# Three stretches of a matmul-bound attention and expert kernel: the second unit's weight blocks earlier, the last unit's sums in another order, the result's last blocks in pieces

## The chip, the cores and the metric

The kernel runs on one core of a Trainium2 chip, all in float32. The metric is the time of one execution in microseconds (us), the median of several runs. PE is the TensorE engine, PEld its weight loads, DVE VectorE, ACT ScalarE, POOL GpSimd, SP SyncE, whose queue issues most transfers. All runs quoted here are of the fast state. Even so, the kernel before varies: 1200.2 to 1209.1 us over the calls. Each kernel is therefore compared with runs of the kernel before on the same chip in the same call.

## The reference

```python
# cut to what matters
for b in range(nb):                      # 12 chunks of 64 positions, 4 batches, 8 heads
    intra = (q_b @ k_b.T * lam ** (i - j) (i >= j)) @ v_b
    inter = (q_b * lam ** (pos + 1)) @ kv_state
    out_b = intra + inter
    kv_state = lam ** 64 * kv_state + (k_b * lam ** (63 - pos)).T @ v_b
x = out as (3072, 512)                   # rows by model width
p = domain_probs / sum
out = sum over the 4 experts e of  p[:, e] * (relu(x @ w1[e]) @ w2[e])
```

## The kernel before

The rows of x fall into 3 groups, with 4 experts each: 12 units of work. The first unit's products are formed directly as soon as the attention of the first group is done ("direct products", 56 to 92 us). From the second unit on, each product of x with w1 (line of pg) is interleaved with a product of the hidden values with w2 (line of q). The products are of Strassen's kind with seven terms M1 to M7, each fed with sums and differences of blocks. DVE and POOL make these operand sums; DVE also adds up PSUM banks ("evictions"), and PE can use a bank again only then.

Engines work through their queues in order. The program is written by a Python scheduler: `chores` are side jobs, of which `pump` takes one when its count of steps says that POOL is free. The place in the program where a chore is written settles where its instructions stand in every engine's queue.

```python
def load(n, names="qkv"):                       # one chunk of q, k, v
    ...
    for r in range(2):
        nc.sync.dma_start(out=to[:, :, r], in_=of[:, :, r])
lam_bc = consts.tile([P, H], FP32, name="lam_bc")
nc.scalar.dma_start(out=lam_bc[:], in_=lam.partition_broadcast(P))
... # DVE makes s_decay (8 scans) and q_decay (7 products) of lam_bc;
    # st = scores * s_decay feeds PE's product with v

stage = ctx.enter_context(tc.tile_pool(name="stage", bufs=8))   # operand tiles, tag "st"

def pump(pace=1.0, force=False):
    ...                                          # stores that are due
    begins = chores and (force or free[0] <= now[0])
    if begins:
        begin = free[0] = max(free[0], now[0] - 1)
        was = max(busy[0], now[0])
        chores.pop(0)()
        free[0] = max(free[0], begin + max(pace * (busy[0] - was), 1))

def own_x(m):        # second unit: x operands of product m, four sums on DVE
    ...
    for n, x, y, op in T_OPS:
        tt(nc.vector, b[n], b[x], b[y], op)
    keep_own(("x", 0, m), x_ops[0, MS.index(m)], pieces)      # store for later groups
def own(m):          # own_w1: the same for w1, on POOL
    fed[0, 1, m] = own_x(m), own_w1(m)

raws = [lambda n=n: raw_w1(1, n) for n in ("A11", "A12", "A21", "A22")]
chores.extend((*prepare_w2(1), *raws, pause(4), mine["M1"], sum_own("S1", "A21", "A22", ALU.add)))
...                  # then the direct products, with pump() in every step
chores.extend((
    mine["M5"], sum_own("S2", "S1", "A11"),
    pause_till(0, 4), mine["M6"], sum_own("S3", "A11", "A21"),
    pause_till(1, 4), mine["M2"], sum_own("S4", "A12", "S2"),
    pause_till(2, 4), mine["M7"], ... ))
...
def give(m, t, tags):                            # turns a block of the result back
    ...                                          # 4 transposes into one bank
    nc.scalar.copy(out=o[:], in_=p[:])
    nc.sync.dma_start(out=out[r:r + 256, ...], in_=...)
```

## Time and profile before

| | before |
|---|---|
| median of the first 3 runs | 1204.43 us (1203.54 to 1204.65) |
| span of the profiled run | 1202.6 us |
| PE busy | 1188.0 us (99%) |
| PE not busy | 14.6 us |
| granted clock | 1.00 from the first record at 6.90 us to 1201.56 us, but for one stretch of 0.5, 95.65 to 99.06 us |

A table of windows has a row for each stretch: its length, the busy time and the number of instructions of PE, PEld, DVE, ACT and POOL, the granted clock, the share of the transfer engines, GB/s. A timeline's row is start, duration, engine, line, what it makes of what, sizes, count; in brackets stands the idle time before it and what ended that. The prediction below shows the rows that matter.

In what follows "wait" also stands for a figure that I count from the start times of the matmuls: the distance to the next start less the usual one (0.216 us for 128x256). Both kernels have 6623 matmul records of the same shapes in the same order, so the n-th of one can be set against the n-th of the other. I call the difference of their starts the **offset**.

### The profile page before, as it was taken

What the parts mean: (1) busy time and instruction counts of PE and PEld (TensorE: products, weight loads), DVE (VectorE), ACT (ScalarE), POOL (GpSimd) and SP (SyncE); (2) the same over time, 40 slices, a digit from 0 to 9 for tenths busy, and PEclk for the clock granted to TensorE, in tenths of its full rate; (3) what the DMA queues carried; (4) which work ended last, traced back from release to release, by engine and by line L of the source; (5) the groups of instructions that cost most, each with busy time, mean ns of one, the idle gap of its engine ahead of it and who ended that gap; (6) DMA issues with size and microseconds to landing.
All of it is one profiled execution on the core that took longest, in us unless ns stands there. A gap on an engine that the chain in (4) does not pass through costs nothing.

```text
span 1202.6 us, 17908 instructions
## 1 busy us (share of the span) xinstructions
PE 1188.0 (99%) x6623; PEld 1031.2 (86%) x6623; DVE 793.2 (66%) x1318; ACT 261.9 (22%) x476; POOL 635.3 (53%) x600
## 2 busy tenths in 40 slices
PE   9999999999999999999999999999999999999988
PEld 8887888888888888888888888888888888888877
DVE  6597796477467656746755774764665667777774
ACT  3321122112112201311220120120133341241232
POOL 1874267355468800044425745416675774874873
PEclk9999999999999999999999999999999999999999
DMA  9874869999989985789987999898987566566542
GB/s 224 231 262 166 276 208 352 352 315 332 377 286 328 339 286 173 224 286 275 283 286 233 304 311 319 278 315 304 301 280 262 215 229 248 218 241 227 208 151 71
DMA packets 227447, 317.94 MB, mean 264 GB/s; under 512 B 91648, under 2 KB 168864, under 8 KB 227360
## 3 DMA queue, kind: packets, MB, share of 16 engines
q1 hardware_dynamic: 219920, 314.63, 77.6%
q10 hardware_dynamic: 7440, 2.17, 0.8%
q8 instruction: 52, 0.85, 0.3%
q14 instruction: 35, 0.29, 0.1%
HBM read 231.40 MB, written 85.34 MB: 263 GB/s over the span
## 4 chain that ended last, share of the span: by engine, by line
PE 90%; DVE 3%; SPq 3%; DMA 2%; POOL 1%; issue 1%; ACT 0%; DVEq 0%; POOLq 0%
PE pg L733 38%; PE q L787 33%; PE pq L958 12%; DVE m L95 2%; SPq L122 2%; PE sp L484 1%; PE op L512 1%; POOL w2o L95 1%; PE op L507 1%; PE qp L461 1%; PE kp L461 1%; PE pM L928 1%; DMA probs<-in_moe_domain_probs_dram 1%; DMA w1b<-in_moe_w_dram 1%; PE op L520 1%
## 5 line engine op out<-in xcount | busy, mean ns | idle before, releaser
L733 PE MATMUL pg<-xs_in,ws_in 128*128 128x256 f32 x1960 | 470.3, 380 | 0.7 <-DVE m L95 0.5
L733 PEld LDWEIGHTS pg<-xs_in,ws_in 128*128 128x128 f32 x1960 | 370.5, 190 | 53.9 <-DVE m L95 2.5
L95 DVE TENSOR_TENSOR m<-pg,m 128x512 f32<-128x512 f32 x451 | 307.7, 687 | 111.7 <-PE pg L733 101.5
L787 PE MATMUL q<-w2t,hS 128*128 128x256 f32 x1024 | 243.3, 380 | 0.0
L787 PEld LDWEIGHTS q<-w2t,hS 128*128 128x128 f32 x1024 | 192.9, 190 | 26.8 <-issue 0.3
L803 DVE SCALAR_TENSOR_TENSOR acc<-q,gate,acc 128x256 f32<-128x256 f32 x192 | 92.4, 481 | 174.0 <-PE q L787 173.1
L787 PE MATMUL q<-w2t,m 128*128 128x256 f32 x768 | 183.9, 383 | 0.0
L787 PEld LDWEIGHTS q<-w2t,m 128*128 128x128 f32 x768 | 145.9, 191 | 20.6 <-issue 0.2
L745 ACT ACTIVATE m<-m 128x512 f32<-128x512 f32 x132 | 83.0, 630 | 337.1 <-DVE m L95 335.3
L95 POOL TENSOR_TENSOR m<-m,xT 128x512 f32<-128x512 f32 x64 | 81.6, 1290 | 78.4 <-ACT m L745 46.3
L95 POOL TENSOR_TENSOR kn<-kn,s_decay 128x512 f32<-128x512 f32 x20 | 22.1, 1105 | 170.4 <-PE kp L461 130.3
L95 DVE TENSOR_TENSOR sums<-pq,sums 128x256 f32<-128x256 f32 x154 | 64.1, 421 | 49.3 <-PE pq L958 41.7
L958 PE MATMUL pq<-acc,w2t 128*128 128x256 f32 x352 | 86.7, 379 | 1.9 <-POOL acc L95 1.9
L741 ACT COPY m<-pg 128x512 f32<-128x512 f32 x88 | 51.4, 585 | 154.6 <-PE pg L733 147.9
L95 DVE TENSOR_TENSOR m<-m,m 128x512 f32<-128x512 f32 x96 | 81.0, 847 | 0.0
L95 POOL TENSOR_TENSOR ops<-w2b 128x256 f32<-128x256 f32 x24 | 18.9, 807 | 109.6 <-DMA w2b<-in_moe_w_dram 109.6
L958 PEld LDWEIGHTS pq<-acc,w2t 128*128 128x128 f32 x352 | 66.8, 190 | 11.3 <-issue 2.2
L680 ACT ACTIVATE m<-m 128x512 f32<-128x512 f32 x48 | 30.3, 631 | 154.0 <-DVE m L95 154.0
L95 DVE TENSOR_TENSOR hS<-m,m 128x512 f32<-128x512 f32 x64 | 54.8, 861 | 8.4 <-ACT m L745 8.4
L95 POOL TENSOR_TENSOR acc<-hT,hT 128x512 f32<-128x512 f32 x32 | 40.1, 1270 | 32.5 <-DVE hT L95 19.5
L95 POOL TENSOR_TENSOR w2o<-w2b 128x512 f32<-128x512 f32 x32 | 41.8, 1326 | 24.2 <-DMA w2b<-in_moe_w_dram 21.4
L95 POOL TENSOR_TENSOR acc<-hT,acc 128x512 f32<-128x512 f32 x32 | 40.7, 1271 | 5.0 <-PE pq L958 2.7
(129 smaller groups left out, 1325.5 us busy)
## 6 DMA issues: line engine op xcount, KB each, us to landing
xs_in<-x_ops SPq DMA_DIRECT2D x70, 896.0 KB, 6.0
ws_in<-w_ops SPq DMA_DIRECT2D x70, 896.0 KB, 8.6
w2t<-w_ops SPq DMA_DIRECT2D x66, 256.0 KB, 6.6
w2t<-w_sums SPq DMA_DIRECT2D x64, 256.0 KB, 3.8
w_ops<-ops SPq DMA_DIRECT2D x28, 512.0 KB, 5.4
w2t<-in_moe_w_dram SPq DMA_DIRECT2D x48, 256.0 KB, 3.3
x_ops<-ops SPq DMA_DIRECT2D x17, 512.0 KB, 6.8
w2b<-in_moe_w_dram SPq DMA_DIRECT2D x32, 256.0 KB, 5.7
```

The source lines that it names most:

```text
L95: eng.tensor_tensor(out=o, in0=a, in1=b, op=op)
L122: nc.sync.dma_start(out=to[:, :, r], in_=of[:, :, r])
L461: nc.tensor.transpose(out=x[:, ac * C:(ac + 1) * C], in_=y[:, 2 * ac:2 * ac + 2].rearrange("p r d -> p (r d)"), identity=ident[:],)
L484: nc.tensor.matmul(out=sp[r][:, ac * C:(ac + 1) * C], lhsT=hc(kT)[half[r], ac], rhs=hc(qT)[half[r], ac], start=True, stop=True,)
L507: nc.tensor.matmul(out=op[r][half[x], a * C:(a + 1) * C], lhsT=kv[half[r], 2 * a + x], rhs=hc(qs)[half[r], 2 * a + x], start=(a == 0), sto ...
L680: nc.scalar.activation(out=o[:], in_=o[:], func=AF.Relu)
L733: nc.tensor.matmul(out=p[:, j * 256:(j + 1) * 256], lhsT=ws[i][:, j * P:(j + 1) * P], rhs=xs[i], start=(fresh and j == 0), stop=True, skip ...
L741: nc.scalar.copy(out=new[at][:], in_=p[:])
L745: nc.scalar.activation(out=new[at][:], in_=new[at][:], func=AF.Relu)
L787: nc.tensor.matmul(out=p[:, s * DH:(s + 1) * DH], lhsT=h[A_OF[m]][:, c * 256 + s * P:c * 256 + (s + 1) * P], rhs=fed2[g, e, m][uu][:, c], ...
L803: nc.vector.scalar_tensor_tensor(out=o, in0=x, scalar=w, in1=o, op0=ALU.mult, op1=ALU.add)
L958: nc.tensor.matmul(out=p[:, 0:256], lhsT=fed3[e, m, x // 2][:, x % 2, c * P:(c + 1) * P], rhs=b[B_OF[i]][:, c * 256:(c + 1) * 256], start= ...
```

## The change

The intent: the blocks of w1 for the second unit are asked for during the attention, so that its first product doesn't wait at 92 us; the last unit's operand sums are made in an order that fits its short products; the last blocks of the result go out in smaller pieces. With it comes a fourth edit: half of the first q and k loads go to ACT's queue, and lam_bc is asked for behind them.

```diff
@@ part A: load, lam_bc
                 for r in range(2):
-                    nc.sync.dma_start(out=to[:, :, r], in_=of[:, :, r])
+                    by = nc.scalar if n < 2 and r == 1 else nc.sync
+                    by.dma_start(out=to[:, :, r], in_=of[:, :, r])
-    lam_bc = consts.tile([P, H], FP32, name="lam_bc")
-    nc.scalar.dma_start(out=lam_bc[:], in_=lam.partition_broadcast(P))
...
+    lam_bc = consts.tile([P, H], FP32, name="lam_bc")
     for n, names in ((0, "qk"), (1, "qk"), (0, "v"), (2, "qk"), (1, "v"), (3, "qk")):
         load(n, names)
+        if (n, names) == (1, "qk"):
+            nc.scalar.dma_start(out=lam_bc[:], in_=lam.partition_broadcast(P))
@@ part B1: second unit (cut: the tiles of block A21 and of sum S1 also leave the stage buffers)
-            chores.extend(prepare_w2(0))
+            chores.extend((*prepare_w2(0), *(raw[n] for n in ("A11", "A22", "A21"))))
...
-    chores.extend((*prepare_w2(1), *raws, pause(4), mine["M1"], sum_own("S1", "A21", "A22", ALU.add)))
+    chores.extend((
+        mine["M1"], sum_own("S1", "A21", "A22", ALU.add), *prepare_w2(1), raw["A12"],
+    ))
@@ part B2: last unit (cut)
+        for part in names:            # outer sums: T1 of all blocks first, then T3 and T2
+            for at in BLOCKS:
...
+            b[name] = small("h" + name) if (e, m) == EARLY else opool.tile([P, W], FP32, name="acc")
...
-                elif ahead or x % 2 == 0:
+                elif ahead or x % 2 == 0 and x + i:
                     rest()
@@ part C: result (cut)
-    def give(m, t, tags):
+    def give(m, t, tags, dds=(0, 1)):
...
-    "M4": (("M5", 0), ("M5", 1), ("M2", 0), ("M2", 1), ("M4", 0))
+    "M4": (("M5", 0), ("M5", 1), ("M2", 0), ("M2", 1), ("M4", 0, (1,)), ("M4", 1, (1,)))
-    give("M4", 1, ("s1",))
+    give("M4", 0, ("q01",), (0,))
+    give("M4", 1, ("q11",), (0,))
```

More of the change, by code (lines that the diff above doesn't have):

```diff
@@ L333, in raw_w1 @@
         i, j = int(name[1]) - 1, int(name[2]) - 1
-        if name == "A22":
+        if name in ("A21", "A22"):
             to = tuple(small("w1b")[:] for _ in range(2))
@@ L344, in sum_w1 @@
     def sum_w1(e, name, a, b, op):
-        if e == 0:
+        if e == 0 or name == "S1":
             to = tuple(small("w1o")[:] for _ in range(2))
@@ L440, in take @@
         for x, f in enumerate(queue):
-            if force or getattr(f, "at", 0) <= now[0]:
+            if force or getattr(f, "at", 0) <= now[0] and getattr(f, "can", lambda: True)():
                 queue.pop(x)()
@@ L617, in total, with inner_sums @@
             outer[e][name][at] = o
-        work = []
-        for at in BLOCKS:
-            for n in names:
-                a, _ = of[n]
-                k = len(work)
-                if n in ("T1", "T3", "T4"):
-                    x = lambda a=a, at=at, tag={"T1": "s0", "T3": "s1", "T4": "s" + "01"[k % 2]}[n]: bring(a, at, tag)
-                    if not work:
-                        work.append([x])
-                    else:
-                        work[-1].append(x)
-                work.append([lambda n=n, at=at: total(n, at)])
-        background.extend(after(6, lambda fs=fs: [f() for f in fs]) for fs in work)
-    def inner_sums(e, m):
+        work, tags = [[]], itertools.cycle(("s0", "s1"))
+        for part in names:
+            for at in BLOCKS:
+                for n in part:
+                    if n != "T2":
+                        work[-1].append(lambda a=of[n][0], at=at, tag=next(tags): bring(a, at, tag))
+                    work.append([lambda n=n, at=at: total(n, at)])
+        background.extend(after(4 + 2 * (i > 4), lambda fs=fs: [f() for f in fs]) for i, fs in enumerate(work))
+    EARLY = E - 1, "M3"
+    def inner_sums(e, m, behind=False):
+        if (e, m) in within:
+            return
         blk, b = outer[e][B_OF[m]], {}
@@ L642, in total @@
                 b.update({"B" + at: blk[at] for at in BLOCKS})
-            b[name] = opool.tile([P, W], FP32, name="acc")
+            b[name] = small("h" + name) if (e, m) == EARLY else opool.tile([P, W], FP32, name="acc")
             tt(nc.gpsimd, b[name][:], b[x][:], b[y][:], ALU.subtract)
-        aside[0:0] = [lambda n=n, x=x, y=y: total(n, x, y) for n, x, y, _ in T_OPS]
+        work = [after(0, lambda n=n, x=x, y=y: total(n, x, y)) for n, x, y, _ in T_OPS]
+        for f in work:
+            f.can = lambda: len(blk) == 4
+        if behind:
+            aside.extend(work)
+        else:
+            aside[0:0] = work
     SEQ = ("M1", "M5", "M6", "M2", "M7", "M3", "M4")
@@ L690, in keep @@
             if g == LAST:
-                outer_sums(e, *{(0, 1): ("T1", "T3", "T2"), (1, 0): ("T4",)}.get((i, j), ()))
+                outer_sums(e, *{(0, 1): (("T1",), ("T3", "T2")), (1, 0): (("T4",),)}.get((i, j), ()))
                 return
@@ L904, in give @@
         p, o = bank(tags[t % len(tags)], "yp"), small("y")
-        for dd in range(2):
+        w = len(dds) * P
+        for x, dd in enumerate(dds):
             for s in range(2):
                 nc.tensor.transpose(
-                    out=p[:, s * DH + dd * P:s * DH + (dd + 1) * P], in_=sums[m][:, 2 * dd + t, s * P:(s + 1) * P],
+                    out=p[:, s * w + x * P:s * w + (x + 1) * P], in_=sums[m][:, 2 * dd + t, s * P:(s + 1) * P],
                     identity=ident[:],
                 )
-        nc.scalar.copy(out=o[:], in_=p[:])
-        r = LAST * G + j * W + t * 256
+        nc.scalar.copy(out=o[:, 0:2 * w], in_=p[:, 0:2 * w])
+        r, d = LAST * G + j * W + t * 256, i * DH + dds[0] * P
         nc.sync.dma_start(
-            out=out[r:r + 256, i * DH:(i + 1) * DH].rearrange("(s p) d -> p s d", p=P),
-            in_=o[:].rearrange("p (s d) -> p s d", s=2),
+            out=out[r:r + 256, d:d + w].rearrange("(s p) d -> p s d", p=P),
+            in_=o[:, 0:2 * w].rearrange("p (s d) -> p s d", s=2),
         )
@@ L1074 @@
     blocks = {}
+    raw = {n: lambda n=n: raw_w1(1, n) for n in ("A11", "A12", "A21", "A22")}
     m1, m2 = (direct_product(0, m, blocks, ("g1", "g3")) for m in ("M1", "M2"))
@@ L1134, in sum_own @@
         return lambda: sum_w1(1, name, a, b, op)
-    raws = [lambda n=n: raw_w1(1, n) for n in ("A11", "A12", "A21", "A22")]
-    chores.extend((*prepare_w2(1), *raws, pause(4), mine["M1"], sum_own("S1", "A21", "A22", ALU.add)))
+    chores.extend((
+        mine["M1"], sum_own("S1", "A21", "A22", ALU.add), *prepare_w2(1), raw["A12"],
+    ))
     for m in SEQ0[2:]:
@@ L1167 @@
     fill3 = [(e, m, k) for e in range(E) for m in SEQ3 for k in range(4)]
-    after_last = {"M2": (None,) * 5 + (("M3", 0), ("M3", 1)), "M4": (("M5", 0), ("M5", 1), ("M2", 0), ("M2", 1), ("M4", 0))}
+    after_last = {
+        "M2": (None,) * 5 + (("M3", 0), ("M3", 1)),
+        "M4": (("M5", 0), ("M5", 1), ("M2", 0), ("M2", 1), ("M4", 0, (1,)), ("M4", 1, (1,))),
+    }
     steps = attention(1)
@@ L1201 @@
             if nests and i == 6:
-                inner_sums(ahead[1], SEQ3[0])
+                inner_sums(ahead[1], SEQ3[0], nested)
+                if ahead[1] == EARLY[0]:
+                    inner_sums(*EARLY, True)
             a = []
@@ L1228 @@
                     if y:
-                        give(*y, ("s0", "s1"))
+                        give(*y[:2], ("s0", "s1"), *y[2:])
                 if x == 0 and at * 7 + i >= 6 and fill:
```

## The prediction

> **What bounds the kernel now.** I read the busy line first, then the waits of TensorE (PE), then a table of windows, then timelines of the stretches that the change touches. The page's busy line:
>
> ```profile
> PE 1188.0 (99%) x6623; PEld 1031.2 (86%) x6623; DVE 793.2 (66%) x1318; ACT 261.9 (22%) x476; POOL 635.3 (53%) x600
> ```
>
> and three rows of the waits (us in total, times, longest):
>
> ```profile
> PE pg L733 <- DVE ops L95: 2.9, 1, 2.9
> PE pq L958 <- POOL acc L95: 1.9, 1, 1.9
> PE yp L907 <- DVE sums L95: 1.2, 2, 0.6
> ```
>
> PE is busy for 1188.0 of a span of 1202.6 us. So **all waiting of PE together is 14.6 us**, 1.2% of the time; only a change of the matmuls, or of their clock, could bring more. The order listing shows PE's instructions in the same order in both kernels, 6623 of them, so the matmul work stays. 2% of 1204.43 is 24.1 us, which is more than all that could be saved.
>
> Where the 14.6 us lie, by windows (length, then busy time of PE, PEld, DVE, ACT, POOL, then granted clock, DMA share, GB/s):
>
> ```profile
> 0.00:20.00 20.00, 18.94 (x209) 17.43 (x210) 14.79 (x31) 7.27 (x13) 4.95 (x10) 1.00 0.92 223
> 60.00:80.00 20.00, 20.00 (x94) 17.61 (x93) 19.86 (x24) 1.17 (x2) 15.68 (x12) 1.00 0.88 310
> 80.00:100.00 20.00, 17.13 (x73) 14.44 (x72) 18.04 (x29) 8.44 (x14) 11.13 (x8) 0.91 0.46 149
> 1140.00:1160.00 20.00, 17.05 (x77) 13.97 (x76) 15.78 (x32) 7.44 (x13) 14.69 (x13) 1.00 0.52 190
> 1180.00:1200.00 20.00, 17.54 (x96) 14.84 (x94) 9.94 (x19) 6.78 (x12) 3.91 (x4) 1.00 0.26 92
> ```
>
> The idle time is at the start (1.06 us), at 80 to 100 us (2.87), at 1140 to 1160 (2.95) and at the end (2.46, and the 2.6 after 1200 us). The change works on just these. In 80 to 100 the clock is 0.91 as well, so that window loses more than its idle time. The timeline of PE there (start, us, out<-in, idle before):
>
> ```profile
> 89.36 1.89 PE L787 MATMUL q<-w2t,m 128*128 128x256 f32 x8
> 91.08 1.03 PE L733 MATMUL pg<-xT,w1b 128*128 128x256 f32 x4
> 94.98 1.40 PE L733 MATMUL pg<-ops 128*128 128x256 f32 x4 [2.87 <-DVE ops L95]
> 96.17 3.32 PE L787 MATMUL q<-w2t,m 128*128 128x256 f32 x8
> ```
>
> Eight matmuls of one kind took 1.89 us before the gap and 3.32 after it; start to start, 91.08-89.36 = 1.72 us against 99.33-96.17 = 3.16 (99.33 is the start of the next group). With the four of 94.98 I count **1.7 us lost to the clock after 2.87 us of idle time**. The operands come late because VectorE (DVE) has no idle time from 57 to 97 us and runs its queue in order:
>
> ```profile
> 94.42 0.75 DVE L95 TENSOR_TENSOR ops<-xT 128x256 f32<-128x256 f32 x2
> ```
>
> At the start, the lines that decide are of DVE, and PE's first product that needs them:
>
> ```profile
> 3.85 2.63 DVE L380 TENSOR_TENSOR_SCAN s_decay<-lam_bc,ident 128x128 f32<-128x128 f32 x8 [2.86 <-DMA lam_bc<-in_lam_dram]
> 6.76 3.43 DVE L393 TENSOR_TENSOR q_decay<-q_decay 128x4 f32<-128x4 f32 x7
> ...
> 10.90 1.28 DVE L95 TENSOR_TENSOR st<-sp,s_decay 128x512 f32<-128x512 f32 x2
> ```
>
> and of PE:
>
> ```profile
> 12.54 1.09 PE L512 MATMUL op<-st,vn 128*64 128x128 f32 x16
> ```
>
> From the landing of lam_bc DVE works without a break to 12.18, and PE takes up st 0.4 us later: **this chain has no slack today**.
>
> **What the Trainium skill says.**
> - "TensorE: Matmul & The Clock Gate", the section on the clock gate: PE is at half rate after at least one idle window, and the window is 3413 ns and free-running. The trace agrees on the length (records of the granted clock show 0.5 from 95.65 to 99.06, 3.41 us), less on the condition: the gap was 2.87 us, shorter than a window. The gap of 2.0 us at 1147 left the clock at 1.00.
> - "DMA: Bandwidth & Descriptors", "Anatomy of one DMA": about 2.0 us fixed for each DMA. Here lam_bc, 4 KB, took 3.0 us from issue to landing; the last output blocks take about 2.4.
> - "Trainium Kernel Development and Optimization", "Key Constraints": queues of SP and ACT use the same 16 engines, so a second queue only saves issue time. In 0 to 20 us the DMA share is 0.92 and SP spends about 0.55 us on each issue, so part A can speed up only the first issues.
> - "GPSIMD Engine Reference", its table of specifications: POOL shares SBUF interfaces with DVE, for DVE instructions of two SBUF inputs. Here one such 128x512 sum takes 0.64 us with POOL idle and 1.72 with it busy.
>
> **Part A, the start: half of the first q and k loads on ACT's queue, lam_bc behind them.** The change's title leaves it out, but it matters. Before, lam_bc was issued first on ACT (0.73) and landed at 3.76. After, four loads stand before it there. The program shows that the DMAs share eight semaphores in turn; lam_bc is the ninth and waits for the first q load, which lands at about 4.0 (3.94 before). Its own 3.0 us put it at 7.1 to 7.4, **3.4 us later**. The DVE chain follows: s_decay from 7.2, st finished at 12.18+3.4 = 15.6, perhaps 15.0 as the scores it had to wait for come earlier. The first values product starts at 15.0 to 15.6 instead of 12.54. What PE has before it ends some 0.6 us earlier, as the loads land earlier, so PE stands for about 3.3 us; the end moves by +2.6. The loads land earlier by 0.6 to 0.8, so the waits for qn and kn near 21 us (0.39 and 0.64 in the gap list) go: -1.0. A gap of over 3 us may halve the clock for 3.4 us (+1.7); it hangs on how it falls on the grid of windows, even odds, my guess. **Sum: +1.6, or +3.3 with the drop.**
>
> **Part B1, the second unit's w1 blocks in the attention.** The blocks are now issued at about 54 us instead of 69.5 and land by 63.5; POOL's sums for the first product follow at 61 to 64. DVE's four own operand sums (1.65 us) stand 29 instructions earlier in its order, so ready near 76, against need at 92. This removes the 2.87 us and the 1.7 us of half clock: **-4.6**. Moved the other way: the w2 blocks of the second expert now stand on SP's queue behind a store that waits for those sums, so they are issued near 77 to 84 and land near 88, against need at 89.4: 1 to 4 us of slack. DVE's total work stays, and POOL is moved off the stretch where DVE is full, so PE's PSUM banks should come free in time; the least slack of such a bank near 72 us is 0.2 us.
>
> **Part B2, the last unit's sums.** Two gaps in the timeline of PE are meant:
>
> ```profile
> 1146.77 1.03 PE L958 MATMUL pq<-acc,w2t 128*128 128x256 f32 x4
> 1149.65 2.61 PE L958 MATMUL pq<-acc,w2t 128*128 128x256 f32 x11 [1.85 <-POOL acc L95]
> ```
>
> Four matmuls need 0.86 us, so 1149.65 is 2.0 late. The profile names POOL's acc; the same instruction also waits for a DVE sum that frees its bank, which stands behind an hT sum that waits for ACT's copy (1147.91 to 1148.49). After, POOL's sums are taken about 4.5 us earlier and DVE's order has the eviction earlier: I walk it with the same durations to 1148.4, -1.2. The gap of 1.23 at 1155.55 is DVE's eviction behind four hT sums, now taken elsewhere: -1.2. The 0.72 at 1162.95 keeps its order in both. **Sum: -2.4.**
>
> **Part C, the last blocks in pieces.** The wait of 0.77 us at 1195.04 (a transpose for a block just summed) goes, as half of it was turned before. After the last sum 2+2 transposes and two copies of 256 columns (0.37 each, estimated from the 0.59 for 512) stand in place of 4 and one of 0.59: -0.15, and one more DMA follows, landing as before after 2.4 us. **Sum: -0.9.**
>
> **Sum:** -4.6-2.4-0.9+1.6 = -6.3 without the drop of the clock at the start, -4.6 with it. I allow +0.5 for new waits, and get -5: 1199.5 us.
>
> **Rivals.**
> 1. The late lam_bc costs as much as the repair at 92 us brings: a gap of 4 us and the half clock, +5. For it: the chain has no slack. Against: PE has transposes and scores of the next blocks only up to about 12 us, which bounds it at 3.3. Time near 1202.
> 2. A new wait at 89 to 100 us takes the place of the old: w2 lands late behind the store, or DVE, full from 57 to 97, frees a bank late. For it: 19.86 of 20 us busy. Against: 29 places of lead and less POOL beside it. Time 1201 to 1203.
> 3. lam_bc lands sooner than I think (its semaphore free early), no stall: all of 7.9+1.0 us comes. The rotation of semaphores speaks against it. Time 1195.5.
>
> **Range and chances.** All rivals lie within 1195.5 and 1203, so 8 in 10 for 1196 to 1203.5. Faster by over 2% would need more than PE's whole idle time, slower by over 2% a stall of 24 us; 0.01 each.
>
> **What the profile would show.** Part A: s_decay starting near 7.2 instead of 3.85 and op near 15 with about 3 us idle before; the clock under 1.00 in 0 to 20 if it drops. B1: the ops before 80 us, no idle before pg<-ops, clock 1.00 in 80 to 100. B2: PE near 19.4 busy in the window 1140 to 1160. C: no wait of yp in its middle, last landing about 0.15 us sooner after the last sum. I am wrong if s_decay still starts near 4, or PE idles for over 1 us between 60 and 100 us on w2t, m or PSUM.

## The result, and the profile after

The changed kernel took 1206.71 us (median; 1205.87 to 1207.42, 4 runs), the kernel before 1204.54 (1203.54 to 1206.29, 4 runs). The ratio is 1.0016, 95% interval 0.9999 to 1.0034: no gain, rather a loss of 2 us, where 1199.5 was expected and 1203.5 was the upper end of the range. A ratio is the mean time of one kernel's fast runs over that of the other's of the same rounds, so not quite the ratio of the medians.

The windows of the changed kernel, for the stretches where the prediction saw idle time, and two more:

```profile
0.00:20.00 20.00, 13.89 (x122) 12.65 (x124) 10.75 (x24) 5.25 (x9) 3.79 (x9) 0.88 0.91 223
20.00:40.00 20.00, 20.00 (x244) 17.23 (x243) 11.15 (x17) 6.46 (x15) 11.07 (x9) 0.95 1.00 256
...
80.00:100.00 20.00, 20.00 (x94) 17.61 (x93) 17.14 (x28) 8.68 (x14) 3.33 (x3) 1.00 0.93 298
100.00:120.00 20.00, 18.78 (x87) 15.88 (x86) 15.21 (x22) 2.93 (x5) 17.13 (x16) 1.00 0.63 209
...
1140.00:1160.00 20.00, 19.46 (x89) 16.48 (x88) 15.77 (x31) 7.27 (x13) 19.69 (x17) 1.00 0.60 218
```

In 80 to 100 us PE is now busy throughout at full clock, and in 1140 to 1160 for 19.46 instead of 17.05 us: there the change does what it should. Of the two gaps in the last unit one of 0.5 us is left:

```profile
1154.76 2.83 PE L965 MATMUL pq<-acc,w2t 128*128 128x256 f32 x12 [0.51 <-POOL m L95]
```

But the first window has 13.89 us instead of 18.94, and the clock is below 1 in two windows. In 100 to 120 us, where the kernel before had no idle time, 1.2 us is new. The waits of PE (us in total, times, longest) name three things that are new or, like the second, far longer (0.5 us in all before):

```profile
PE op L513 <- DVE st L95: 5.0, 1, 5.0
PE pg L739 <- DVE m L95: 4.3, 7, 1.7
...
PE pg L739 <- POOL ops L95: 0.9, 1, 0.9
```

The start. DVE's timeline, then PE's first product with st:

```profile
8.07 2.63 DVE L381 TENSOR_TENSOR_SCAN s_decay<-lam_bc,ident 128x128 f32<-128x128 f32 x8 [7.08 <-DMA lam_bc<-in_lam_dram]
...
10.97 4.25 DVE L394 TENSOR_TENSOR q_decay<-q_decay 128x4 f32<-128x4 f32 x7
...
15.94 1.28 DVE L95 TENSOR_TENSOR st<-sp,s_decay 128x512 f32<-128x512 f32 x2
```

```profile
16.68 2.15 PE L513 MATMUL op<-st,vn 128*64 128x128 f32 x16 [4.97 <-DVE st L95]
```

The scans of s_decay start at 8.07 instead of 3.85. lam_bc was issued at 3.84, when the first load's semaphore was free, as expected, but needed 4.13 us to land instead of 3.0, with seven other loads on their way. The q_decay chain took 4.25 instead of 3.43 us. One of its products takes 0.17 to 0.42 us when POOL is idle, but 0.95 to 1.16 when a POOL product of 1.06 us has just begun beside it; of these POOL ran three beside the chain, from 10.84 to 13.93 us, and two in the kernel before. The same 16 products that took 1.09 us now take 2.15: half clock, from 15.10 to 21.93 us by its records.

The new waits at 104 to 155 us. Of these the longest, in the timelines of DVE and PE:

```profile
125.31 2.10 DVE L95 TENSOR_TENSOR ops<-xT 128x256 f32<-128x256 f32 x2
127.45 1.83 DVE L95 TENSOR_TENSOR ops<-xT,ops 128x256 f32<-128x256 f32 x2
129.20 1.28 DVE L95 TENSOR_TENSOR m<-pg,m 128x512 f32<-128x512 f32 x2
```

```profile
126.44 1.89 PE L793 MATMUL q<-w2t,hS 128*128 128x256 f32 x8
130.03 1.10 PE L739 MATMUL pg<-xt,ops 128*128 128x256 f32 x4 [1.70 <-DVE m L95]
```

PE needs the bank that the eviction at 129.20 frees. The four sums for product M2 (ops), which PE needs only some 12 us later, stand ahead of it and take 3.9 us together, with POOL at work beside them (until 128.54); in the kernel before they take 1.65. The kernel before has the same instructions in another order there:

```profile
122.84 0.69 DVE L95 TENSOR_TENSOR m<-pg,m 128x512 f32<-128x512 f32 x1 [0.38 <-PE pg L733]
123.70 0.69 DVE L95 TENSOR_TENSOR m<-pg,m 128x512 f32<-128x512 f32 x1 [0.17 <-PE pg L733]
...
125.83 0.75 DVE L95 TENSOR_TENSOR ops<-xT 128x256 f32<-128x256 f32 x2
```

Both evictions come first, and the first two of the sums take 0.75 us. In DVE's queue, the sums for M6, M2, M7 and M3 begin at places 130, 139, 154 and 179 before, and at 126, 136, 148 and 172 after.

SP's timeline shows something else that the chores' order did:

```profile
61.80 0.43 SPq L1032 DMA_DIRECT2D x_ops<-xT  x1
77.21 0.32 SPq L1032 DMA_DIRECT2D x_ops<-ops  x1
77.57 0.43 SPq L1032 DMA_DIRECT2D x_ops<-xT  x1
78.05 2.09 SPq L238 DMA_DIRECT2D w2b<-in_moe_w_dram  x1
```

The store of M1's x sums blocks the queue for 15 us, until DVE has made them, and the loads of w2 for the second expert behind it start at 78.05 instead of 52.93. POOL's timeline gives what follows:

```profile
84.49 3.30 POOL L95 TENSOR_TENSOR w2o<-w2b 128x512 f32<-128x512 f32 x2 [15.38 <-DMA w2b<-in_moe_w_dram]
99.97 2.96 POOL L95 TENSOR_TENSOR w2o<-w2b 128x512 f32<-128x512 f32 x2 [12.18 <-DMA w_sums<-w2o]
```

POOL is idle for 15.4 and 12.2 us, and its work piles up after 100 us.

The ledger by offsets (after less before, one profiled run each):

| stretch | step | offset after it |
|---|---|---|
| full clock from 4.86 us on instead of 6.90 | -0.92 | -0.92 |
| wait for st at 11.4 us | +5.06 | +4.14 |
| half clock until 21.9 us | +2.36 | +6.50 |
| waits for qn, kn near 21 us gone | -0.93 | +5.57 |
| first direct product on xt | +0.33 | +5.90 |
| wait and half clock at 92 to 99 us gone | -4.71 | +1.19 |
| new waits at 104 to 160 us | +4.91 | +6.10 |
| 160 to 424 us | +0.52 | +6.62 |
| 424 us to the last unit (-2.54 at 1147 and 1155 us) | -2.70 | +3.92 |
| result turned back | -0.91 | +3.01 |

The first row is not a matter of waiting for loads. Four transposes of the same kind at the start, in the kernel before and in the changed one:

```profile
5.48 1.06 PE L461 MATMUL qp<-ident,qn 128*128 128x128 f32 x4
5.19 0.60 PE L462 MATMUL qp<-ident,qn 128*128 128x128 f32 x4
```

Up to the first record of a granted clock the matmuls start 0.214 us apart, after it 0.11: PE begins at half rate, and the windows' clock of 1.00 doesn't show that. The first record stands at 6.90 us before and at 4.86 after, and the lead grows by 0.10 us with each matmul just there. In the five traces with the first loads of the kernel before it stands between 4.60 and 7.28 us, in those with the change's loads (this one, fill_start and fill_22) at 4.16 to 4.86, in the other eight at 5.13 to 7.00. PE does the same work up to there in all of them, so I take this lead for luck; three traces don't show it. What earlier loads can do is keep such a lead: x_mid below (4.60 us) loses its 0.94 us in waits for kn at 7.6 and 11.4 us.

### The profile page after: what moved, and what is told of

Read it like the earlier page. It is cut to its first block, busy times and chain, and to the rows that moved or that the text cites. A ratio compares the mean times of both kernels' runs of the same rounds, so it can differ in the third digit from the quotient of the medians.

```text
span 1205.6 us, 17896 instructions
## 1 busy us (share of the span) xinstructions
PE 1188.2 (99%) x6623; PEld 1031.1 (86%) x6623; DVE 797.2 (66%) x1318; ACT 261.6 (22%) x478; POOL 634.0 (53%) x600
## 4 chain that ended last, share of the span: by engine, by line
PE 92%; DVE 4%; POOL 2%; DMA 1%; issue 1%; ACT 0%; SPq 0%; ACTq 0%; DVEq 0%; POOLq 0%
PE pg L739 37%; PE q L793 31%; PE pq L965 12%; PE pM L1050 4%; PE op L513 2%; PE sp L485 2%; DVE m L95 1%; PE op L508 1%; PE op L521 1%; PE qp L462 1%; PE kp L462 1%; PE pM L935 1%; DVE ops L95 1%; POOL m L95 1%; DVE xt L95 1%
```

## The experiments

My theory after this: the late lam_bc costs 5.6 us, the new waits at 104 to 155 us cost 4.9 and undo part B1, and parts B2 and C gain 3.5. For the waits there were two rivals at first, the blocked SP queue and the stage buffers; a third, DVE's order, came up with the second set of traces.

All kernels were correct. The columns "waits" are my sums of PE's waits over 0.25 us between 104 and 160 us.

| run | median us (runs) | ratio to before, 95% interval | waits 104 to 160 us |
|---|---|---|---|
| changed kernel | 1206.71 (4) | 1.0016 (0.9999 to 1.0034) | 4.9 |
| lam_first | 1201.41 (21) | 0.9980 (0.9972 to 0.9988) | 4.9 |
| held_store | 1200.55 (10) | 0.9975 (0.9964 to 0.9985) | 3.6 |
| only_w1_early | 1206.42 (12) | 1.0024 (1.0015 to 1.0034) | 4.8 by offset |
| only_last_unit | 1199.64 (5) | 0.9966 (0.9953 to 0.9979) | as before |
| sums_behind | 1206.67 (18) | 1.0020 (1.0011 to 1.0029) | 3.0 |
| held_behind | 1204.97 (14) | 1.0012 (1.0002 to 1.0022) | 1.9 |
| x_early | 1200.22 (8) | 0.9965 (0.9953 to 0.9978) | 0.3 |
| fill_start | 1210.05 (6) | 1.0051 (1.0035 to 1.0067) | 4.9 |
| x_mid | 1197.59 (6) | 0.9945 (0.9926 to 0.9964) | 0.3 |
| x_mid_spread | 1198.12 (14) | 0.9949 (0.9933 to 0.9966) | 0.3 |
| fill_22 | 1205.24 (14) | 1.0007 (0.9997 to 1.0017) | 4.9 |
| nine_stages | 1206.52 (22) | 1.0024 (1.0014 to 1.0034) | 2.9 and half clock |
| order_back | 1198.49 (6) | 0.9949 (0.9936 to 0.9961) | 0.8 |
| order_back_held | 1197.59 (5) | 0.9940 (0.9928 to 0.9952) | 0.3 |

### lam_first

```diff
 # changed kernel
+    nc.scalar.dma_start(out=lam_bc[:], in_=lam.partition_broadcast(P))
     for n, names in ((0, "qk"), (1, "qk"), ...):
         load(n, names)
-        if (n, names) == (1, "qk"):
-            nc.scalar.dma_start(out=lam_bc[:], in_=lam.partition_broadcast(P))
```

> The changed kernel with one edit: lam_bc asked for first on ACT's queue again, the four spread q and k loads stay. Theory (the late lam_bc costs all of the loss at the start: 5.1 us of waiting for st and 2.4 us of half clock): s_decay starts near 4 instead of 8.07, op near 12.5 instead of 16.68, granted clock 1.00 in 0 to 20 us, time about 6.3 us below the changed kernel, near 1200.5. Rival (later stages are paced by transfers and GpSimd, so an earlier start is lost again in the waits at 110 to 160 us): these waits grow by some us and the time stays above 1203.

Measured: 1201.41 us, 5.3 below the changed kernel's median; by the ratios, 0.36% or 4.3 us. lam_bc landed at 4.27, PE was busy for 18.57 us of the first 20 and the clock was 1.00 there. At 90 us the offset to the kernel before was within 0.3 us of zero. So the late lam_bc is shown to be the whole loss at the start, and spreading the loads alone brought nothing by then. The waits at 104.7, 112.8, 122.0, 134.3 and 152.9 us stayed as they were (1.02, 0.53, 1.84, 0.79, 0.70), neither more nor less: the rival, that an earlier start is eaten by them, is out.

### held_store

```diff
 # lam_first; own_x of M1: the sums where they were, their store later
-        keep_own(("x", 0, m), x_ops[0, MS.index(m)], pieces)
+        keep = lambda: keep_own(("x", 0, m), x_ops[0, MS.index(m)], pieces)
+        held.append(keep) if m == "M1" else keep()
...
-        mine["M1"], sum_own("S1", ...), *prepare_w2(1), raw["A12"],
+        mine["M1"], sum_own("S1", ...), *prepare_w2(1), raw["A12"], lambda: held.pop()(),
```

> lam_first with one more edit: the store of the first product's x operands is asked for only after the second expert's w2 work, so it does not stand ahead of those loads in SP's queue. Theory (SP stood 15 us for that store, w2b came at 78 instead of 53 us, and GpSimd's work piled up at 100 to 128 us): w2b issued near 62, no idle time of GpSimd of 15 us before its first w2 sum, PE's waits between 104 and 155 us together under 1.5 us, time 4 us below lam_first, near 1196.5. Rival (the eight stage buffers are what GpSimd waits for: its second w2 sum takes the buffer of the first one's store, the third that of the operands PE reads near 92 us): GpSimd still idles until over 90 us, the waits at 104 to 155 stay over 3 us, time within 1.5 us of lam_first.

Measured: 1200.55 us, 0.9 below lam_first (0.6 by the ratios, whose intervals overlap), far from the 4 us expected. SP did issue w2b at 57.7 us and POOL's first w2 sum came at 66.48, so the blocked queue was real. It was not what made most of the waits; 3.6 us of them stayed, with one of 2.2 us at 131.6. POOL's next w2 sum shows that the rival has a point as well:

```profile
81.35 2.97 POOL L95 TENSOR_TENSOR w2o<-w2b 128x512 f32<-128x512 f32 x2 [11.65 <-DMA w_sums<-w2o]
```

It waited for the store of the first one, whose buffer it takes.

### only_w1_early

The kernel before with the hunks of part B1.

> The kernel before with part B1 alone (second unit's w1 blocks and operand sums early). Theory (B1 removes 4.6 us at 92 to 99 us and brings new waits of about 4.7 us at 104 to 155 us): within 1 us of the kernel before, 1204 to 1205; no wait before pg<-ops, clock 1.00 in 80 to 100, and PE busy under 19.0 in 100 to 120 or 120 to 140. Rival (the new waits come from the late start, which shifts the attention against the loads): waits stay away, 4.6 us faster, 1199.9.

Measured: 1206.42 us, ratio 1.0024, so part B1 alone loses 2.9 us and is worse than the nothing that the theory gave it. By offsets, it gains 4.8 us at 92 to 96 us and loses 4.9 from there to 155, as the theory has it. The rest of what the profiled run is behind (4.0 us) lies elsewhere: 1.5 us before 90 us, nearly all in waits for kn and qn at 11 to 24 us, ahead of anything that part B1 moves, 0.4 in small steps after 155 us, and 2.0 at the end, where the old wait near 1149 us was 2.36 us long and was followed by half clock from 1153.30 to 1156.71. The waits came without the late start, so the rival is out.

### only_last_unit

The kernel before with the hunks of parts B2 and C.

> The kernel before with parts B2 and C alone (last unit's sums reordered, last blocks in pieces). Theory: the waits of 2.0 and 1.2 us near 1147 and 1155 shrink to under 0.8 together (-2.6 us) and one of the two of 0.77 at the end goes (-0.8): 1201.0, 3.4 us below the kernel before. Rival (the gain at 1147 only shows because the late start moved transfers): under 1.5 us.

Measured: 1199.64 us, ratio 0.9966, 4.1 us faster. By offsets -2.5 at 1147 and 1155 us and -0.9 at the end. These parts are worth what was predicted, by themselves.

### sums_behind and held_behind

```diff
 # lam_first (sums_behind), held_store (held_behind)
-        pause_till(0, 4), mine["M6"], ...     pause_till(1, 4), mine["M2"], ...
-        pause_till(2, 4), mine["M7"], ...     pause_till(3, 4), mine["M3"], ...
-        pause_till(4, 4), mine["M4"], ...
+        pause_till(0, 14), mine["M6"], ...    pause_till(1, 9), mine["M2"], ...
+        pause_till(2, 9), mine["M7"], ...     pause_till(3, 8), mine["M3"], ...
+        pause_till(4, 8), mine["M4"], ...
```

> lam_first with VectorE's own operand sums of the second unit's products (M6, M2, M7, M3) taken later, at places 130, 141, 154 and 182 of its order, near those of the kernel before (130, 139, 154, 179) instead of 126, 136, 148 and 172; the store stays where the change has it. Theory (these sums now stand ahead of evictions that PE's next product needs, and this makes most of the 4.7 us of new waits): the waits between 104 and 155 us are together under 1.7 us, time 3 us below lam_first, near 1198.5. Rival (GpSimd's own lateness makes them): they stay over 3.5 us, now on GpSimd's ops, time within 1 us of lam_first.

> held_store and sums_behind together (places 130, 141, 154, 182). If order and the store are both causes and add: waits between 104 and 155 us under 0.8 us in all, time near 1196.5. If the store alone still matters nothing once the order is mended: as sums_behind, 1198.5. If a third cause remains (the stage buffers, GpSimd's speed): waits of over 2 us stay, 1199 or more.

Measured: 1206.67 and 1204.97 us, both slower than what they were built on. The waits at 113, 122 and 153 us went, but the one at 134 grew to 1.9, and a new one of 5.5 us appeared at 390 us: six sums of hidden values (hS), 0.8 to 1.6 us each with POOL beside them, in front of an eviction, followed by half clock. My edit had delayed POOL's sums and the third expert's steps together with DVE's sums. These two runs decide nothing between the rivals, except that such a wait can be made elsewhere in the same way.

### x_early and x_mid

```diff
 # the kernel before with parts B2 and C; held as in held_store
+    w2_work = prepare_w2(1)
-    chores.extend((*prepare_w2(1), *raws, pause(4), mine["M1"], sum_own(...)))
+    chores.extend((w2_work[0], early_x, *w2_work[1:], *raws, pause(4), late_w1, sum_own(...)))      # x_early
+    chores.extend((*w2_work[:5], early_x, *w2_work[5:], *raws, pause(4), late_w1, sum_own(...)))    # x_mid
 # early_x: own_x("M1"); late_w1: the held store, then own_w1("M1")
```

> The kernel before with parts B2 and C, and of B1 only one thing: the four sums of VectorE for the second unit's first product stand earlier in its order (71 instead of 104), their store and all loads and GpSimd's work stay where they were. Theory (the wait at 92 us was VectorE's order alone; the blocks of w1 were never late): no wait at 92, clock 1.00 in 80 to 100, no new waits at 104 to 155, time 4.6 us below only_last_unit, near 1195.5. Rival (the four sums, put into a stretch where VectorE has no idle time, push the evictions of the direct products): 1 to 1.7 us of PE waiting between 60 and 92 us, time 1197 to 1198.

> As x_early, with the four sums at place 90 of VectorE's order instead of 71: the trace of the kernel before leaves 2.9 to 5.7 us there between an eviction and the product that needs its bank, against 0.25 us near place 72. All loads and GpSimd's work stay as in the kernel before. Theory (the wait at 92 us was VectorE's order alone, and the wait of 2.3 us at 72.8 us of x_early came from the place): no wait over 0.5 us between 60 and 100 us, clock 1.00 in 80 to 100, no new waits at 104 to 155 us; time 4.6 us below only_last_unit, near 1195.2. Rival (GpSimd's load beside VectorE stretches the sums anyway): a wait of over 1 us between 72 and 93, time over 1197.

Measured: x_early 1200.22 us, no better than only_last_unit (1199.64). The wait at 92 us was gone and clock 1.00, but a new one stood at 72.8 us:

```profile
75.37 2.86 PE L1051 MATMUL pM<-xt,w1o 128*128 128x256 f32 x12 [2.18 <-DVE m L95]
```

That is the rival that was named: the sums were put where an eviction had 0.25 us to spare, and with POOL at work beside them they took 4.75 us there instead of the 1.65 counted on. With the sums at place 90, x_mid took 1197.59 us, ratio 0.9945. Its window:

```profile
80.00:100.00 20.00, 20.00 (x94) 17.52 (x93) 19.90 (x32) 8.84 (x15) 11.19 (x9) 1.00 0.54 181
```

PE has no idle time and full clock there, with every load and all POOL work in the order of the kernel before; the blocks of w1 landed from 75.1 to 83.7 us (76.2 to 83.2 before). So the wait at 92 us is shown to have been DVE's order alone; the blocks of w1 were never late. The time came out 2.4 us above the 1195.2 expected. In the traces x_mid is 3.8 us ahead of only_last_unit: 4.6 are gained at 92 to 99 us, and some 0.9 lost again near 413 us, mostly in a wait for ws_in. The profiled run (span 1194.9) also has three waits for kn of 1.5 us in all at the start. The rest isn't explained.

### x_mid_spread

x_mid with the load hunk of part A and lam_bc first, as in lam_first.

> x_mid with half of the first q and k loads on ACT's queue and lam_bc still first there. Theory (the sixteen transfer engines are busy for 0.92 of the start, so spreading the issues brings little, and what it brings VectorE's chain eats): within 0.5 us of x_mid. Rival (the waits for qn and kn near 21 us go): 1 us faster than x_mid.

Measured: 1198.12 us, ratio 0.9949 against 0.9945: no difference, as the theory has it. The waits near 21 us shrank to one of 0.48, but the runs spread from 1194.4 to 1203.2.

### fill_start and fill_22

```diff
 # changed kernel
             if i < 2 and lag == 0:
                 warm(3 - i)
+            if i == 2 and lag == 1:
+                warm(44)          # fill_22: warm(22)
```

> The changed kernel with 44 idle products (on zeros, result not used) put into PE's wait for st at the start, about 4.7 us of work. Theory (the half clock after 16 us follows from the 5 us of idle PE): clock 1.00 in 0 to 20 and 20 to 40, op still starts near 16.7, time 2.4 us below the changed kernel, near 1204.3. Rival (the clock is low there for another reason, or the late start is paid back later anyway): time as the changed kernel, 1206.7.

> The run fill_start with 22 idle products instead of 44: the 44 took 10.1 us (two passes each), 5 us more than the wait had. Theory (the half clock follows from the idle PE): the 22 fill 5.0 us, op starts near 16.7, clock 1.00 from 7 to 40 us, time 2.4 us below the changed kernel, near 1204.3. Rival (the low clock costs nothing that would not be lost later): as the changed kernel, 1206.7.

Measured: fill_start is a miss of mine. Each such float32 product is recorded as two passes, so 44 took 10.1 us and PE reached op at 21.66; time 1210.05 us. The 22 of fill_22 fit: 5.18 us from 11.60, op at 16.71, and the clock stayed at 1.00 in both windows:

```profile
0.00:20.00 20.00, 18.77 (x182) 17.25 (x183) 11.57 (x26) 5.44 (x9) 3.79 (x9) 1.00 0.97 235
20.00:40.00 20.00, 20.00 (x250) 17.19 (x249) 12.06 (x19) 7.47 (x16) 10.70 (x9) 1.00 0.92 234
```

Set against the changed kernel, the matmuls run level at op (+0.03) and 2.39 us ahead at 62 us. So the half clock followed from the idle time and cost 2.4 us. The median is 1205.24, 1.5 below the changed kernel's, on another chip and in another call; in the traces 2.9.

### nine_stages

```diff
 # held_store
-NPOOL = 47
+NPOOL = 45
-    stage = ctx.enter_context(tc.tile_pool(name="stage", bufs=8))
+    stage = ctx.enter_context(tc.tile_pool(name="stage", bufs=9))
```

> held_store with nine stage buffers instead of eight (and 45 small tiles instead of 47, to make room); VectorE's order is that of held_store. Theory of the buffers (GpSimd's second w2 sum stood 11.65 us for the store of the first to land because no other buffer was free): GpSimd goes on at 69.7, has no idle time before 80 us, its sums for the second product are done before 88 us instead of 95.7; the waits between 104 and 155 us shrink from 3.8 to under 2.5 us. If only VectorE's order makes them: they stay at 3.6 us or more, and time within 0.7 us of held_store (1200.5). GpSimd will now run beside VectorE's full stretch of 70 to 85 us, so a new wait of PE there of up to 1.5 us may take back the gain.

Measured: 1206.52 us, 6 us slower than held_store. POOL did go on without the buffer. It then was busy for 18.76 us of 60 to 80, beside DVE's fullest stretch, and PE stood there for 3.0 us:

```profile
60.00:80.00 20.00, 17.00 (x75) 14.49 (x74) 19.79 (x22) 0.69 (x2) 18.76 (x15) 0.93 1.08 377
```

Half clock followed from 77.17 to 84.00 us. In 100 to 120 us POOL was busy for 5.75 us only, and in 120 to 140 for 4.27; still the waits of 2.2 us at 136 and 0.7 at 158 were there. So GpSimd's lateness isn't what makes these two, and the stage buffers aren't either. (The 4.27 us do lie beside DVE's sums before the first of them, four in 2.73 us; the wait was followed by half clock from 138.61 to 142.02.) That left DVE's order, which sums_behind had not changed cleanly.

### order_back and order_back_held

```diff
 # lam_first (order_back), held_store (order_back_held)
     def own(m):
-        fed[0, 1, m] = own_x(m), own_w1(m)
+        b = own_w1(m)
+        def x():
+            fed[0, 1, m] = own_x(m), b
+        late.append((now[0] + LATE[m], x)) if m in LATE else x()
+    # LATE = M6 3, M2 2, M7 3, M3 3 steps (held: 2, 1, 2, 2); pump() takes what is due in late first
```

> lam_first with VectorE's own sums for M6, M2, M7 and M3 alone taken 2 to 3 steps later, so that VectorE's order from place 120 to 190 is that of the kernel before (130, 139, 154, 179); GpSimd's order is that of lam_first, line for line. Theory (order): of the waits of lam_first at 104.7 (1.02, on GpSimd's ops), 112.8 (0.53), 122.0 (1.84), 134.3 (0.79) and 152.9 (0.70) only the first and one of 0.3 to 0.6 at 134 stay, 1.5 us in all instead of 4.9: time 3.3 us below lam_first (1201.4), near 1198. Rival (GpSimd's late work beside VectorE stretches sums and evictions in any order): over 2.9 us stay, as in sums_behind, time within 1.5 us of lam_first.

> order_back with the held store of held_store, so that GpSimd's sums for the second product are ready at 96 instead of 107 us. If order and the store are the two causes: no wait over 0.4 us between 104 and 155 us, under 0.8 us in all; time near 1197, where x_mid is (1197.6). If the wait of 2.2 us at 131 to 136 us of held_store and nine_stages has a third cause: it stays over 1.5 us and the time is over 1198.5.

Measured: 1198.49 and 1197.59 us. The windows of order_back:

```profile
100.00:120.00 20.00, 19.68 (x91) 17.01 (x91) 14.87 (x21) 2.93 (x5) 19.53 (x21) 1.00 0.83 277
120.00:140.00 20.00, 19.87 (x96) 17.26 (x96) 15.41 (x29) 1.70 (x3) 6.67 (x7) 1.00 0.61 223
```

With GpSimd's order that of lam_first, line for line, and POOL busy for 19.53 of 20 us, PE's waits at 104 to 160 us fell from 4.9 to 0.8 us (0.48 at 105.0, 0.29 at 135.0), just by DVE's own sums standing behind the evictions again. PE's, ACT's and GpSimd's instructions are those of lam_first in the same order; besides DVE's order only that of some stores on SP's queue moved along. The sums for M6 in DVE's timeline:

```profile
113.78 0.69 DVE L95 TENSOR_TENSOR m<-pg,m 128x512 f32<-128x512 f32 x1 [0.17 <-PE pg L742]
114.39 3.83 DVE L95 TENSOR_TENSOR xt<-xt 128x256 f32<-128x256 f32 x4
```

With POOL beside them they take 3.83 us, as long as those for M2 in the changed kernel, but behind the eviction no wait of PE follows. The time fell by 2.9 us against lam_first, though a wait of 1.2 us at 190 us is new. The order of DVE's queue is thereby shown to be the cause of the waits. What POOL's work adds to their length in the bad order no run separates; by the lengths (3.9 against 1.65 us) I estimate that the longest, 1.86 us, would hardly have been there without it. Holding the store as well takes away the rest of these waits: 0.29 us in all, as in only_last_unit; time 1197.59 us. This is the changed kernel with its faults mended, and it ends level with x_mid (1197.59), which leaves the loads alone.

## Why the prediction was wrong

The prediction's sum was -4.6 - 2.4 - 0.9 + 1.6 and room for new waits. Step by step:

- **What bounds the kernel**: right. PE's matmul work stayed, busy 1188.2 against 1188.0 us.
- **Part A**: the mechanism was right, its size was not. "3.4 us later" for lam_bc measured 4.2 (8.07 - 3.85): the step took 3.0 us for the transfer from the kernel before, where only one load was asked for at the same moment, and it took 4.1 with seven on their way. The DVE chain was taken over at its old length and grew by 0.8 with a third POOL product beside it. So PE stood for 5.1 instead of 3.3 us and op moved by 4.14, not 2.6. The half clock, given even odds and 1.7 us, came, for two windows, and cost 2.36. In sum +5.57 instead of +1.6 or +3.3, and that with a lead of PE of 0.9 us before the wait, which the prediction had as 0.6 "as the loads land earlier" and which came from the earlier full clock, probably by luck. Rival 1 named this, but "bounds it at 3.3" was the error.
- **Part B1**: the gain was right to 0.1 us (-4.71 against -4.6) in the profiled pair. The step that failed is the sentence "DVE's total work stays, and POOL is moved off the stretch where DVE is full, so PE's PSUM banks should come free in time". It looked at the direct products up to 100 us and at amounts of work. What was moved with the chores was the place of the sums for M6, M2, M7 and M3 in DVE's queue, 3 to 7 places ahead, in front of evictions. This cost 4.9 us at 104 to 160. Rival 2 had the kind of wait ("frees a bank late") and gave 1201 to 1203 for it; it put it at 89 to 100 us, and the prediction allowed 0.5 us for all new waits. The order listing, which I had, shows these places; I used it for PE and for M1's sums, not for these.
- **The w2 loads** behind the store: seen, and the first w2 product was indeed in time, at no cost at 89 to 100 us. What POOL's delay costs by itself is small: 0.9 us by the medians (lam_first to held_store, or order_back to order_back_held), and in both pairs the intervals overlap.
- **Part B2**: -2.70 by offset against -2.4, right. **Part C**: -0.91 against -0.9, right; the pair alone gave -4.1 us in time.
- **The range**: the two misses, +2.3 to +4.0 and +4.9, add to one side, and rivals 1 and 2 were taken as alternatives. Both came true together, and that lies above 1203.5.

Two things stay open. Part B1 alone is 2.9 us slower in time, where its offsets at 92 to 155 us all but cancel; the waits at the start and the half clock at the end of its one trace were not followed through its other runs. And x_mid, at 1197.59 us, is 2.4 us above the sum of its parts. One reason is on record: the half clock does not fall alike in every run. Of the 124 runs of the kernel before, 32 have a mean clock of 1.000 and take 1202.5 us on average; 54 have 0.998, like the profiled one with its half clock at 95.65 us, and take 1204.9. So what half clock cost in one trace is not lost in every run. Where it fell in the runs without a trace is not known.

## What to carry to other kernels

When a change moves side work earlier, compare the order of every engine's queue, not only of the engine that bounds: a sum that nobody needs yet costs the full wait if it stands in front of the eviction that the bounding engine waits for. Before moving transfers, ask whether the late operand was late for its data or for its place in a queue: here four sums moved from place 104 to place 90 did the work of all of part B1. And a tiny transfer at the head of a long serial chain is asked for first, whatever large loads stand beside it.

## What the Trainium skill lacked or had wrong

- "TensorE: Matmul & The Clock Gate", the section on the clock gate, gives half rate after at least one idle window of about 3.4 us. Here shorter waits sufficed: 3.03 us (before), 2.70 (only_last_unit), 2.36 (only_w1_early) and 2.21 (nine_stages) were followed by half clock, while 2.02 (before), 2.21 (held_store) and 2.35 (x_early) were not. Every half-clock stretch between the first and the last record lasted 3.41 or 6.83 us, one or two windows, as the page's window length has it; waits of 3.2, 5.1 and 5.5 us brought two (nine_stages, changed kernel, sums_behind), another of 5.5 us one (held_behind).
- "DMA: Bandwidth & Descriptors" has no figure for a small transfer of ACT's queue among large ones; its section "Anatomy of one DMA" is about GpSimd's queue. From issue to landing the 4 KB of lam_bc took 3.0 to 3.1 us when asked for first with the loads on SP's queue alone, 3.4 to 4.0 when asked for first with the loads on both queues, and 3.7 to 4.1 behind four loads of ACT's queue.
- None of the pages that I read warns that a DMA issue that waits for a late operand holds up all later issues of its queue: here 15 us of SP's queue, 61.80 to 77.21 us.
